# Nine loads moved from SP's queue to ACT's in a delta-rule attention with a softplus layer behind it

## The chip, the cores and the metric

The kernel runs on one core of a Trainium2 chip. The metric is device time in microseconds (us) of one execution, as the median of several. Beside the times there is one profiled execution, whose trace has every instruction of the five engines (PE for matmuls, DVE, ACT, POOL, and SP, which here only issues DMAs) and the landing of every DMA. Times inside a run are counted from the first instruction of the trace.

## What is computed

Four batches of eight heads go through a recurrence over 768 steps with a 48x48 state per head. The 384 features of each of the 3072 tokens then go through two dense layers with a softplus between them.

```python
k_n = k / (norm(k) + 1e-6)
for t in range(768):                       # q, k, v, g: [4, 8, 768, 48], beta: [4, 8, 768]
    y[:, :, t] = g[:, :, t] * (q[:, :, t] @ state)
    v_old = state^T k_n[:, :, t]
    state = state + beta[:, :, t] * outer(k_n[:, :, t], v[:, :, t] - v_old)
x = y as [3072, 384]
out = softplus(x @ w_in) @ w_out           # w_in: [384, 2048], w_out: [2048, 384]
```

## The kernel before

The 768 steps are cut into 12 chunks of 64, numbered 0 to 11, and all 32 heads are worked on together. For a chunk the kernel needs its keys, queries, values and gates. Each of these four is a tile of 384 KB, brought by two DMAs of 192 KB. Keys, values and gates arrive as 1024 rows of 192 bytes per DMA (`load`, L242 to L259, the DMA itself is at L249), queries as rows of 1536 bytes (`load_q`, L261 to L273, the DMA at L271). They land in rings of buffers: three for keys (`kf`), two for queries (`qf`), three for values (`vf`) and three for gates (`gf`). So a load waits until the last reader of the chunk that had the buffer before is done.

What reads them:

- A key tile is squared on ACT for the norm (`ksq`, L545), summed on DVE (`nv`, L549), and multiplied by the inverse norm on DVE or POOL (`kn`, L327), or only cast, in chunks 0 and 1. PE transposes the result and the query tile (L345, L388), ACT and DVE copy them out of PSUM (`kqt`), and PE multiplies them with each other (L503). ACT and DVE take the products out of PSUM (`kk` copies on ACT at L218, masks `mt` on DVE at L518).
- The inverse of each chunk's triangular matrix is built for two chunks at a time, on POOL for all pairs but the first (L629 to L646), and finished on PE (L707, L732, L770).
- The recurrence (`chain`) takes a value tile: DVE subtracts the readout (`w`, L847), PE multiplies twice (L855 and L878) with ACT or DVE copying in between and after (`u`, L218 or L220), PE updates the state (L898) and forms the output (L813, L928). DVE multiplies by the gate tile (`yg`, L943), PE transposes the product (L962), and ACT or DVE copies it (`xt`).
- The dense layers (`dense`) take `xt`: PE at L992, softplus on ACT (`ga`, L1004), PE at L1019, a copy out (`osb`) and the store by SP (L1039).

The weights of the dense layers are loaded by POOL's queue, eight DMAs in all (L297).

The order of everything is written out by hand. Each piece of work is an item with a number, and `_ORDER` is one long list of items, each with a letter for the engine that takes it: P, D, A, G (POOL) or S (SP). `emit` goes through the list once and records each item on its engine. Each engine then runs its own items strictly in that order, and waits between engines are put in where one item needs another's result or buffer. The list therefore fixes the order on each engine, not the times: an engine with little to do runs ahead of the others, as far as the buffers let it.

Loads are items too, eight per chunk: load 8c and 8c+1 are the two halves of the keys of chunk c, 8c+2 and 8c+3 the queries, 8c+4 and 8c+5 the values, 8c+6 and 8c+7 the gates. SP issues all of them but two key halves of chunks 0 and 1, which ACT issues as its first work.

One more rule comes with the recording layer. Loads and stores of SP and ACT count their landings on eight counters, taken in turn. A DMA that takes a counter waits, on the engine that issues it, until the DMA that had the counter before has landed. That one is eight places back among all loads and stores of both queues.

Of the kernel before, what the change touches and what calls it, by code (L numbers as in the profile page):

```python
# [37 lines left out]
class Program:  # L38
# [5 lines left out]
    def add(self, kind, tag, engs, fn, deps=(), bufs=(), mm=0, mode=None, size=0):  # L44
        it = Item()
        it.no, it.kind, it.tag, it.engs, it.fn = len(self.items), kind, tag, engs, fn
        it.deps = [d for d in deps if d is not None]
        it.bufs = list(dict.fromkeys(bufs))
        it.mm, it.mode, it.size = mm, mode, size
        for b in it.bufs:  # L50
            b.users += 1
        self.items.append(it)
        return it
# [21 lines left out]
def kernel(  # L75
# [12 lines left out]
    B, H, S, D = q.shape  # L88
# [19 lines left out]
    add = prog.add  # L108
# [133 lines left out]
    def load(name, x, r, c, b2):  # L242
        if (name, c) not in tiles:
            tiles[name, c] = (Buf(r), [])
        b, its = tiles[name, c]
        t0 = c * C

        def fn(en):
            ENG[en].dma_start(  # L249
                out=b.ap[64 * b2 : 64 * b2 + 64].rearrange("t p h d -> t (p h) d"),  # L250
                in_=x[2 * b2 : 2 * b2 + 2, :, t0 : t0 + C].rearrange(
                    "p h t d -> t (p h) d"
                ),
            )

        its.append(
            add("load", f"{name}{c}.{b2}", "A" if name == "k" and c < 2 and b2 else "S", fn,
                bufs=[b])
        )  # L259

# [14 lines left out]
    for c in range(NC):  # L275
        for b2 in range(2):
            load("k", k, r_k, c, b2)
        for m in range(2):
            load_q(c, m)
        for name, x, r in (("v", v, r_v), ("g", g, r_g)):  # L280
            for b2 in range(2):
                load(name, x, r, c, b2)
# [796 lines left out]
D162 D163 D164 D165 D166 D167 D168 D169 D170 D171 P128 S16 D172 D173 D174 P1251 D175 D176 D177  # L1079
P1244 A197 S25 D198 A222 P223 A224 G179 S11 A140 D178 G238 G239 P1245 A131 P1246 P1247 S24 A199  # L1080
P181 D180 S10 A139 P184 A182 D200 S4 D588 D132 D130 G188 A185 G187 P183 A190 P193 D194 A189 A594
P595 S13 A589 S32 P590 A201 D202 D203 D219 P186 A596 A591 P597 A598 P592 P605 A593 P603 S7 S6
D606 D604 A191 P204 P609 P607 A587 S34 D192 A275 D205 P209 D608 P214 S35 S42 S43 D211 A610 D210
D216 P220 G96 A212 A217 A215 D213 P141 A221 A142 A143 D218 D276 S41 S40 A277 P600 P599 D601 D602
P195 G300 D196 P872 D278 G99 A873 P230 A231 P225 A228 P1255 A226 A233 A235 D232 D229 D227 D611
D234 P874 A875 P886 D236 P619 P612 D620 D613 P151 D155 A284 P884 G98 A887 A885 G97 S14 D237 P285
P1254 A286 P882 P301 A883 A302 P615 A616 S49 P622 A623 P876 S15 A877 P878 G100 G101 G103 P614
P617 G279 D280 P621 P624 D153 S48 A879 A625 A618 G102 D281 P282 D297 P1252 D283 P630 D631 P632
D633 P292 A293 P298 A299 P880 A881 P634 A295 G240 G241 D294 D635 G242 G243 G244 G245 G246 P1253
G247 G248 P303 A304 G249 G250 G251 G252 G253 D306 D307 S50 P308 D296 A309 A311 P904 A905 P916  # L1090
A917 D312 P287 A290 D288 A313 P914 G254 G255 G256 D305 A915 P888 P910 A911 D314 D315 P627 P626
D629 D628 A353 D257 D258 P912 A913 P908 D354 P889 G259 D260 A909 G316 G317 P906 A907 G318 G319
G320 P902 A903 P890 P891 S57 A892 S56 P261 A262 G321 A267 P264 D265 A355 P895 P896 D291 P638
P266 P263 A270 D289 P643 P636 D310 G322 P897 P898 A268 P271 D356 G357 S20 S21 D644 A269 A899
P646 A647 D637 P639 A640 P918 S51 D362 P363 D272 A364 P641 A642 P645 P648 A649 S59 S58 A378 D358
P919 P920 P921 A922 D359 P650 P651 D653 P654 D652 S22 S23 D655 P656 P273 P925 P379 D657 A380
D274 P660 P667 P658 G323 G324 G325 G326 G327 A659 P926 P669 S28 S29 D668 G375 P670 A671 S65 S64
A431 D661 P663 D664 P927 D432 P672 A673 P662 P665 A666 S31 P360 D361 P376 S30 P678 D679 A377
P680 D681 P365 A366 D367 A368 D369 P928 P682 D683 P381 D383 A384 G328 G329 G330 G331 G332 G333
P386 A389 D388 D387 P956 S72 S73 A433 D385 A957 D434 P962 P370 D371 D390 D372 A963 A373 A382  # L1100
# [72 lines left out]
```

## Time and profile before

| what | value |
|---|---|
| median of 3 runs | 257.12 us (254.86 to 260.44) |
| the profiled execution | 255.46 us, of which the span from first to last instruction is 253.6 us |
| busy: PE, DVE, ACT, POOL | 236.9, 153.7, 153.0, 127.1 us |
| loads and stores on SP's queue | 23.2 MB, 50.2% of the 16 DMA engines' time |
| key, value and gate loads, from issue to landing | 3.4 us at least, 5.1 in the middle, 19.5 at most |
| one issue on SP, key loads | 595 ns at least, 639 in the middle, 5067 at most |
| mean granted clock of PE | 0.966 |

The profile's page gives busy times in 40 slices of the span, a digit for each in tenths; the row PEclk has the clock that PE was granted, and the row DMA the share of the DMA engines that was busy. The chain of work that ended last is followed back from the last instruction, at each step to whatever released it. The timelines list instructions by engine in order of time, with the start, the duration, the line, and in brackets the idle time ahead and what ended it. An engine's queue of DMA issues has a q behind its name (SPq, ACTq).

### The profile page before, as it was taken

The numbers are of one execution on the slowest core, as the hardware profiler recorded it, in microseconds if no ns is written. First come the engines' busy times: TensorE is split into PE (matmuls) and PEld (weight loads), VectorE is DVE, ScalarE is ACT, GpSimd is POOL, SyncE is SP. The second block draws the span as 40 slices with busy tenths as digits, with TensorE's granted clock in tenths as the row PEclk, the third lists the DMA queues.
The fourth block names the chain that finished last, engine by engine and source line by source line (L and its number), as shares of the span: only waits on it lengthen the run. The fifth ranks groups of instructions, "written<-read, shape, count | busy, mean of one in ns | idle before, by whom it ended". The sixth has DMA issues, their size and how long they took to land.

```text
span 253.6 us, 11355 instructions
## 1 busy us (share of the span) xinstructions
PE 236.9 (93%) x5040; PEld 160.5 (63%) x5040; DVE 153.7 (61%) x311; ACT 153.0 (60%) x285; POOL 127.1 (50%) x227
## 2 busy tenths in 40 slices
PE   7976588998989999999999999999999999999993
PEld 3543577676766765666766767755676565777751
DVE  7789888775893699759697588523843315313000
ACT  3557777686866579973777675456453475223530
POOL 8201653978879889988948859884000000000000
PEclk9999757799999999999999999999999999999999
DMA  8999999999990789083943850643024130112113
GB/s 111 198 181 178 178 179 180 186 195 176 176 153 6 173 180 157 4 200 83 156 98 84 170 99 22 124 83 80 3 66 93 23 80 0 34 32 48 34 47 78
DMA packets 86192, 27.56 MB, mean 109 GB/s; under 512 B 76288, under 2 KB 86144, under 8 KB 86144
## 3 DMA queue, kind: packets, MB, share of 16 engines
q1 hardware_dynamic: 80096, 23.21, 50.2%
q0 software_dynamic: 3968, 3.25, 8.2%
q10 hardware_dynamic: 2080, 0.39, 1.2%
q8 instruction: 39, 0.64, 1.2%
q14 instruction: 9, 0.07, 0.1%
HBM read 25.26 MB, written 4.72 MB: 118 GB/s over the span
## 4 chain that ended last, share of the span: by engine, by line
PE 76%; DVE 9%; DMA 4%; issue 3%; SPq 2%; ACT 2%; POOL 2%; ACTq 0%; DVEq 0%; POOLq 0%
PE h L992 25%; PE o L1019 23%; PE d L813 4%; DMA beta_l<-in_beta_dram 3%; PE d L855 3%; PE d L732 3%; PE d L770 3%; PE d L878 2%; PE d L928 2%; PE d L503 2%; PE d L707 2%; PE d L898 2%; PE d L388 2%; PE d L345 2%; POOL beta_l L175 2%
## 5 line engine op out<-in xcount | busy, mean ns | idle before, releaser
L1004 ACT ACTIVATE ga<-h 128x512 f16<-128x512 f32 x96 | 56.3, 598 | 33.4 <-PE h L992 27.6
L992 PE MATMUL h<-xt,w_in 128*128 128x512 f16 (+1 forms) x384 | 73.3, 330 | 0.1
L1019 PE MATMUL o<-w_out,ga 128*128 128x384 f16 x384 | 70.3, 326 | 1.4 <-issue 0.7
L1019 PEld LDWEIGHTS <-ga 128*128 128x128 f16 x384 | 35.7, 98 | 23.9 <-issue 1.8
L992 PEld LDWEIGHTS <-w_in 128*128 128x128 f16 x384 | 35.6, 99 | 20.7 <-issue 0.6
L639 POOL TENSOR_TENSOR tmp<-nn,tt 128x30 f32<-128x30 f32 (+7 forms) x75 | 30.1, 401 | 5.6
L646 POOL TENSOR_TENSOR tt<-tt,tmp 128x30 f32<-128x30 f32 (+7 forms) x75 | 29.4, 392 | 5.9
L566 POOL TENSOR_TENSOR nv<-nv,half_c 128x32 f32<-128x32 f32 x4 | 21.8, 5456 | 5.1 <-DVE nv L549 5.1
L218 ACT ACTIVATE kqt<-d 128x1024 f16<-128x1024 f16 (+1 forms) x21 | 18.4, 903 | 7.0 <-PE d L388 6.1
L218 ACT ACTIVATE osb<-o 128x384 f32<-128x384 f32 x18 | 8.8, 489 | 21.5 <-PE o L1019 21.4
L943 DVE TENSOR_TENSOR yg<-d,gf 128x384 f16<-128x384 f32 x24 | 12.8, 553 | 13.6 <-PE d L928 10.2
L1064 PE MATMUL o<-ident 128*128 128x512 f16 x72 | 19.3, 411 | 1.4 <-POOL ident masks.py:199 1.4
L847 DVE TENSOR_TENSOR w<-vf,d 128x384 f16<-128x384 f32 x22 | 11.3, 549 | 12.0 <-PE d L813 10.8
L218 ACT ACTIVATE u<-d 128x384 f16<-128x384 f32 x31 | 14.3, 491 | 7.1 <-PE d L878 3.3
L218 ACT ACTIVATE kk<-d 128x256 f16<-128x256 f32 (+1 forms) x34 | 12.8, 413 | 7.8 <-PE d L503 6.4
L518 DVE TENSOR_TENSOR mt<-d,mask 128x256 f16<-128x256 f32 x40 | 15.5, 418 | 3.2 <-PE d L503 1.9
L220 DVE CAST u<-d 128x384 f16<-128x384 f32 x17 | 9.1, 549 | 13.1 <-PE d L878 11.6
L813 PEld LDWEIGHTS <-kqt 48*64 48x64 f16 x704 | 13.3, 108 | 5.5 <-issue 5.3
L220 DVE COPY osb<-o 128x384 f32<-128x384 f32 x6 | 3.3, 556 | 21.6 <-PE o L1019 21.6
L813 PE MATMUL d<-s,kqt 48*64 48x48 f16 x704 | 16.4, 188 | 0.0
L545 ACT ACTIVATE ksq<-kf 128x768 f32<-128x768 f32 x12 | 10.1, 843 | 7.6 <-DMA kf<-in_k_dram 6.7
L220 POOL CAST tw<-tt 128x256 f16<-128x256 f32 x10 | 5.4, 563 | 16.1 <-DVE tt L646 16.0
(110 smaller groups left out, 380.1 us busy)
## 6 DMA issues: line engine op xcount, KB each, us to landing
qf<-in_q_dram SPq DMA_DIRECT2D x24, 192.0 KB, 5.1
vf<-in_v_dram SPq DMA_DIRECT2D x24, 192.0 KB, 5.2
gf<-in_g_dram SPq DMA_DIRECT2D x24, 192.0 KB, 4.2
out_dram<-osb SPq DMA_DIRECT2D x48, 96.0 KB, 2.4
kf<-in_k_dram SPq DMA_DIRECT2D x22, 192.0 KB, 5.1
w_in<-in_moe_w_in_dram POOLq DMA_DIRECT2D x4, 384.0 KB, 7.5
w_out<-in_moe_w_out_dram POOLq DMA_DIRECT2D x4, 384.0 KB, 12.9
kf<-in_k_dram ACTq DMA_DIRECT2D x2, 192.0 KB, 7.5
```

What stands on the lines that cost most here:

```text
L218: nc.scalar.activation(o, x, AF.Copy, scale=float(sign))
L220: ENG[en].tensor_copy(o, x)
L518: nc.vector.tensor_tensor(mt[c][m].ap[:, NP * p : NP * p + NP], gb[m].ap.rearrange("p (n b) -> p n b", n=NP)[:, :, C:], mask[:, None, :].b ...
L566: lambda en: nc.gpsimd.tensor_tensor(nv.ap, nv.ap, half_c, ALU.pow),
L639: eng.tensor_tensor(t, nn.ap[:, :, j + 1 :, j : j + 1].broadcast_to([P, 2, n, w]), tt.ap[:, :, j : j + 1, :w].broadcast_to([P, 2, n, w]), ...
L646: eng.tensor_tensor(rows, rows, t, ALU.add)
L813: nc.tensor.matmul(hd(o.ap)[HALF[r], NP * p + i], kq_of(c)[FEAT[m], 8 * p + 2 * i + r, off : off + C], s0[r].ap[FEAT[m], NP * p + i], **st ...
L943: lambda en, m=m: nc.vector.tensor_tensor(heads(yg.ap, m), hd(yp[m].ap), heads(gf.ap, m), ALU.mult),
L992: nc.tensor.matmul(hp.ap[:, n * b : n * b + n], w_in[:, j, f * P : (f + 1) * P], xt.ap[:, j, t0 : t0 + n], start=(j == 0), stop=(j == 2),)
L1004: lambda en, hp=hp, o=gb: nc.scalar.activation(o.ap, hp.ap, AF.Softplus),
L1019: nc.tensor.matmul(op.ap[:, :DM], b.ap[:, col + c0 : col + c0 + 128], w_out[:, f, :], start=(f == 0), stop=(f == NF - 1),)
L1064: nc.tensor.matmul(wb.ap.rearrange("p (a b) -> p a b", a=4), ident, ident[:, None, :].broadcast_to([P, 4, P]),)
```

## The change

Nine loads are recorded on ACT's queue in place of SP's. In the list only the letter changes from S to A, the place stays. In the order of the list they are: 32 (keys of chunk 4), 7 (gates of chunk 0), 41 (keys of chunk 5), 15 (gates of chunk 1), 48 (keys of chunk 6), 21 (values of chunk 2), 23 (gates of chunk 2), 29 (values of chunk 3) and 65 (keys of chunk 8). Each is one half of its tile; the other half stays with SP. In `load` the engines that an item may take are widened for this. Nothing else differs: PE, DVE and POOL have the same instructions in the same order, ACT has nine issues more and SP nine fewer. Since the counters are taken in turn over both queues, and the recording layer sorts the issues of the two by its own reckoning, some loads come to wait for another load than before.

```diff
         its.append(
-            add("load", f"{name}{c}.{b2}", "A" if name == "k" and c < 2 and b2 else "S", fn,
+            add("load", f"{name}{c}.{b2}", "A" if name == "k" and c < 2 and b2 else "SA" if c < 9 else "S", fn,
                 bufs=[b])
         )
...
-P595 S13 A589 S32 P590 A201 D202 D203 D219 P186 A596 A591 P597 A598 P592 P605 A593 P603 S7 S6
+P595 S13 A589 A32 P590 A201 D202 D203 D219 P186 A596 A591 P597 A598 P592 P605 A593 P603 A7 S6
 D606 D604 A191 P204 P609 P607 A587 S34 D192 A275 D205 P209 D608 P214 S35 S42 S43 D211 A610 D210
-D216 P220 G96 A212 A217 A215 D213 P141 A221 A142 A143 D218 D276 S41 S40 A277 P600 P599 D601 D602
+D216 P220 G96 A212 A217 A215 D213 P141 A221 A142 A143 D218 D276 A41 S40 A277 P600 P599 D601 D602
...
-P1254 A286 P882 P301 A883 A302 P615 A616 S49 P622 A623 P876 S15 A877 P878 G100 G101 G103 P614
-P617 G279 D280 P621 P624 D153 S48 A879 A625 A618 G102 D281 P282 D297 P1252 D283 P630 D631 P632
+P1254 A286 P882 P301 A883 A302 P615 A616 S49 P622 A623 P876 A15 A877 P878 G100 G101 G103 P614
+P617 G279 D280 P621 P624 D153 A48 A879 A625 A618 G102 D281 P282 D297 P1252 D283 P630 D631 P632
...
-P266 P263 A270 D289 P643 P636 D310 G322 P897 P898 A268 P271 D356 G357 S20 S21 D644 A269 A899
+P266 P263 A270 D289 P643 P636 D310 G322 P897 P898 A268 P271 D356 G357 S20 A21 D644 A269 A899
...
-P919 P920 P921 A922 D359 P650 P651 D653 P654 D652 S22 S23 D655 P656 P273 P925 P379 D657 A380
-D274 P660 P667 P658 G323 G324 G325 G326 G327 A659 P926 P669 S28 S29 D668 G375 P670 A671 S65 S64
+P919 P920 P921 A922 D359 P650 P651 D653 P654 D652 S22 A23 D655 P656 P273 P925 P379 D657 A380
+D274 P660 P667 P658 G323 G324 G325 G326 G327 A659 P926 P669 S28 A29 D668 G375 P670 A671 A65 S64
```

In these lines A277 and A431 are the `ksq` of chunks 5 and 8, D606 and D604 the `yg` of chunk 0, D644 one half of the `w` of chunk 2, and D668 one half of the `w` of chunk 3.

## The prediction

> **What bounds the kernel now.** I read the busy slices first, then the chain that ended last, then the timelines of ACT, DVE and SP around the nine places.
>
> From the page, busy tenths in slices of 6.3 us:
>
> ```profile
> PE   7976588998989999999999999999999999999993
> ...
> ACT  3557777686866579973777675456453475223530
> ...
> PEclk9999757799999999999999999999999999999999
> DMA  8999999999990789083943850643024130112113
> ```
>
> From about 40 us on PE is full to the end: what makes PE wait there is not won back. The DMA engines are full up to 76 us and have room after it.
>
> The chain of work that ended last, in the window 28 to 60 us (start, us, what):
>
> ```profile
> 34.04 0.89 PE d L878 x32
> 34.93 0.02 issue
> 34.95 0.50 ACT u L218
> 35.45 0.33 issue
> 35.78 0.40 DVE yg L943
> ```
>
> ACT's copies of u and the product yg, which reads the gate tile of chunk 0, are themselves on the chain. A load put on ACT's queue in front of them, or a gate that comes late, costs the end directly.
>
> SP's timeline, where the loads are issued (start, us, what):
>
> ```profile
> 25.04 2.10 SPq L249 DMA_DIRECT2D gf<-in_g_dram  x2
> ...
> 33.92 1.33 SPq L249 DMA_DIRECT2D kf<-in_k_dram  x2
> ```
>
> and ACT's timeline beside it:
>
> ```profile
> 34.53 0.92 ACT L218 ACTIVATE u<-d 128x384 f16<-128x384 f32 x2 [0.79 <-PE d L878]
> ...
> 39.95 2.00 ACT L218 ACTIVATE kqt<-d 128x1024 f16<-128x1024 f16 x3
> 41.81 0.86 ACT L545 ACTIVATE ksq<-kf 128x768 f32<-128x768 f32 x1
> ```
>
> This is the heart of it. In the order table load 7 (a gate of chunk 0) stands after the u copies and load 41 (a key of chunk 5) after the kqt copies. SP issues them at 25.04 and 33.92, because SP carries only DMAs and runs ahead of the table. ACT reaches the same places at 35.45 and 41.95. "The same place in the order" is 8 to 20 us later in time.
>
> **What is removed.** Nine issues leave SP, about 0.65 us each (min 595, median 639 to 712 ns): 6 us of a queue that is idle for long stretches. That is worth nothing by itself. SP's later loads move up, but most wait for a buffer (9.2 us once, for DVE's kn), and those waits stay.
>
> **What is added, place by place.** An ACT issue occupies ACT 0.71 to 0.80 us (the two key loads that ACT issues at 1.0 us). From the start of an issue to the landing of the load takes 3.4 us at least, 3.6 for the load at 82.01 into a quiet queue, 4.8 for the one at 33.92, 11.9 for that at 35.30 and 19.5 for that at 38.23, when the weights pass on POOL's queue. A is when ACT gets there in the profile of before, R the first reader and its time.
>
> - Load 32 (key, chunk 4): A 31.6, R ksq 37.23. It lands near 36, in time. Its 0.75 us stand before the sqrt and the u copy at 32.01; the second u copy, which PE needs, loses some 0.5. **+0.5** (0 to 0.8).
> - Load 7 (gate, chunk 0): A 35.45, plus the 0.5 to 0.75 just lost: starts at 36.2. R is yg at 35.78, on the chain. Quiet, it lands at 39.8, by the load at 33.92 at 41.0, by that at 35.30 at 48.1. Weights are moving then: counting packets of 45 to 53 us, SP's queue gets 175 to 203 in a us beside POOL's 179 to 202, and 152 to 177 from 41 to 45; so a load's 1024 packets take 5 to 7 us, after some 2 of start. I take 45: **+9** (4 to 12). Behind yg on DVE stand to, kqt, xt and the masks; PE's transposes of yg (L962, 36.88), next in its order, wait for it, and ACT's xt for those.
> - Load 41 (key, chunk 5): A 41.95, R ksq at 41.81, the very next ACT instruction. ACT itself now sits through the latency: 3.6 quiet, 11.9 at worst. By then, 9.5 us later than now, most of the weights are through; I take **+5.5** (3.6 to 9). Behind it on ACT: the first softplus, then the kk copies that free PSUM for PE.
> - Load 15 (gate, chunk 1): A 54.4, R yg at 57.92, which already waits 1.0 us for it. It lands 3.6 to 4.9 after its issue: **+0.7** (0 to 1.5). Load 48 (key, chunk 6) is read 10 us later: 0.
>
> After 76 us the DMA engines are quiet, so 3.6 counts:
>
> - Load 21 (value, chunk 2): A 75.8, lands 79.4; R w on DVE at 74.73, and PE takes that up at 77.62: **+2.5** (1 to 4.5).
> - Load 23 (gate, chunk 2): A 82.94, lands 86.5; R yg at 83.98. PE's transposes move from 85.59 to 87.6, and ACT's xt from 86.13 to 88.1.
> - Load 29 (value, chunk 3) stands right after that xt: starts at 88.9, lands at 92.5; R w at 85.70, so PE's umm at 86.83 starts at 93.1, and ACT's u copy behind it ends at 94.15 instead of 87.89. It also waits, on ACT, until a load of chunk 9, eight DMAs back, has landed (85.65 now): in time.
> - Load 65 (key, chunk 8) follows that u copy, and ksq is next on ACT: it starts at 94.15, and ksq at 97.75 instead of 87.79. The u copies behind it go from 88.82 to 98.6; PE's L928 at 90.17, which had 0.4 to spare, waits for them. The three loads follow one another, so their delays add: **+9.4** (5 to 12).
>
> **The clock.** PE's granted clock is half from 28.0 to 41.7 us and again from 45.1 to 48.5, after a gap of 1.34 us in PE; that is one step of 3.4 us. In the half step twelve h matmuls took 2.38, outside it six took 0.66. So a step costs up to 1.7 us. Five of the waits above are over 2 us; not all of a step is PE's own time. **+4** (0 to 9). The Trainium skill, "TensorE: Matmul & The Clock Gate" (Part 1, the HAM clock gate), has the same: an idle window of about 3.4 us brings half rate. By its wording gaps shorter than the window would cost nothing, and the term would be near 2; this trace shows a drop after 1.34, so I keep 4.
>
> **The sum.** 0.5 + 9 + 5.5 + 0.7 + 2.5 + 9.4 + 4 = 31.6 us, on the profiled execution's own 255.5 (span 253.6): **287 us**. That execution lies inside the three runs of 254.9 to 260.4, 1.6 under their median; so against the median of 257.1 I say 12% slower. 2%, some 5 us, is what a measurement of this kernel can tell from no change.
>
> **The rivals.**
>
> *The waits overlap or find cover.* All nine latencies are near 3.6, the DVE and ACT delays hide in each other, and the clock stays: 0 + 4 + 3.6 + 0 + 1 + 5 = 13.6, so 269 us; with less still, 262 to 273. For it: ACT is busy 60% and DVE 61%. Against it: after 40 us PE has hardly a gap to hide in.
>
> *Two queues beat one (faster).* Where the weights pass, packets of POOL's queue and SP's alternate one for one. A third queue gets its own share, so keys and gates gain on the weights. The place is 37 to 58 us: the gate issued at 38.23 lands at 57.73, and yg waits 1.0 for it; PE lost 1.34 at 43.36 and 0.71 at 57.20. All of that won is 3 us, and were the half clock of 45 to 48.5 us gone too, 1.7 more: 251. It decides only if a load from ACT lands within 0.3 us of ACT's arrival for load 7 and at once for 41, against the 3.4 us that is the least of all key, value and gate loads. The Trainium skill, "DMA: Bandwidth & Descriptors" (Queues, rings and completion order), has this rule, an engine going round the queues packet by packet; the counts above agree.
>
> *Nothing changes.* The latencies were prefetched far enough, only issue time moves: 255 to 258. The Trainium skill, "DMA: Bandwidth & Descriptors" (Issuing engines are not separate DMA queues), speaks for this: all queues share the 16 engines, and another issuer saves only the sequencer's time. It is silent on what stands behind the issue. The table itself speaks against: for 7, 41, 21, 23, 29 and 65 the reader comes within 2 us of ACT's arrival, or before it.
>
> *Heavier.* Load 7 and 41 each meet the full 12 us of 35.30, the clock takes 9: 0.8 + 12 + 9 + 1.5 + 4.5 + 12 + 9 = 49, so 304.
>
> **The chances.** The forecast (273 to 300) 0.70; overlap (262 to 273) 0.15; heavier 0.07; no change 0.05; faster 0.03. The range of 268 to 302 leaves out both small cases, part of the overlap and the heavy end. Faster by over 2%: 0.03; within 2%: 0.05; slower: 0.92.
>
> **What would show it.** In the profile after: yg's first instruction waits on a DMA of gf for 5 us or more near 36 us; ksq on ACT waits on kf twice, after 41 and near 90 or later, 3 us or more each; w waits on vf twice; ACT's queue issues nine more loads, each soon after the ACT instruction ahead of it; PEclk shows more half steps before 110 us; and from there to the end the two timelines run in parallel. I am wrong if yg of chunk 0 doesn't wait, or if PE finds other work while ACT waits, which its fixed order forbids.

## The result, and the profile after

The changed kernel takes 288.66 us (median of 4 executions, 285.73 to 292.26) against 256.96 us for the kernel before (254.86 to 260.44): 1.123 times the time, with an interval of 1.108 to 1.137. The execution that was profiled took 289.54 us, its span is 287.8 us. That is 34.2 us more span than before. Of every kernel some executions come out a few us longer than the rest: the ratios and the differences in us below leave them out, and so do the times of late4 and splate7, but the traces of late4, three and splate7 are of such executions.

Four parts of the page, first the busy slices (7.2 us each now), then the loads' two queues (packets, MB, share of 16 engines), the chain by engine and the line of DMA issues on ACT's queue:

```profile
PE   8965804689996942599999999999999999999993
...
ACT  3657723386964520269856786753644447423530
...
PEclk9999555859999795569999999999999999999999
DMA  8999799809971497800359637416322413012122
```

```profile
q1 hardware_dynamic: 70736, 21.44, 41.9%
...
q10 hardware_dynamic: 11440, 2.16, 5.0%
...
PE 62%; DMA 16%; POOL 9%; DVE 8%; issue 2%; ACT 1%; DVEq 0%; ACTq 0%; POOLq 0%
...
kf<-in_k_dram ACTq DMA_DIRECT2D x6, 192.0 KB, 5.7
```

The loss stands mostly in two holes of PE's row, slices 6 to 8 and 15 to 17, and in and around each of them the clock is at half. From slice 18 on both kernels are full to the end. DMA holds 16% of the chain. In the kernel before it held 4%, and PE 76%:

```profile
PE 76%; DVE 9%; DMA 4%; issue 3%; SPq 2%; ACT 2%; POOL 2%; ACTq 0%; DVEq 0%; POOLq 0%
```

No byte more is moved: 9360 packets went from SP's queue (q1) to ACT's (q10).

The first hole, in the chain of work that ended last, window 28 to 60 us (start, us, what):

```profile
33.19 0.90 PE d L878 x16
34.09 0.02 issue
34.12 0.01 ACT u L218
34.12 11.24 DMA gf<-in_g_dram
...
45.55 0.06 DVE yg L943
...
50.56 5.95 DMA kf<-in_k_dram
...
56.67 0.85 ACT ksq L545
```

Read it downwards: the u copy starts on ACT at 34.12, load 7 behind it is issued in the same instant, and the next thing that the kernel's end hangs on is its landing 11.24 us later, and then yg. The same again with load 41, 5.95 us, and `ksq`.

The waits in the window 28 to 130 us (who waited for whom; us in total, times, the longest):

```profile
DVE yg L943 <- DMA gf<-in_g_dram: 14.0, 2, 10.5
...
DVE w L847 <- DMA vf<-in_v_dram: 11.0, 2, 6.7
...
PE d L962 <- DVE yg L943: 10.4, 1, 10.4
ACT ksq L545 <- DMA kf<-in_k_dram: 10.3, 2, 5.4
...
PE d L855 <- DVE w L847: 9.0, 2, 6.3
```

In the kernel before only one of these three waits for a DMA was there:

```profile
DVE yg L943 <- DMA gf<-in_g_dram: 1.0, 1, 1.0
```

Since PE executes the same 5040 matmuls in the same order in both kernels, the loss can be followed matmul by matmul: how much later does each start than in the kernel before? This distance is worked out from the two traces, with the times of the kernel before on the left:

```
before, us   matmul                              later by, us
  32.86      umm (L855)                              -0.8
  36.88      transposes of yg, chunk 0 (L962)        +9.8   load 7
  47.27      h (L992)                                +8.6
  47.48      h, waits for ACT's softplus            +10.6   load 41
  51.59      h (L992)                               +13.2   half clock, 0.6 of it softplus
  76.03      o (L1019)                              +12.2
  77.62      umm, chunk 2 (L855)                    +15.1   load 21
  79.42      L878                                   +16.5   half clock
  85.28      behind the transposes of yg, chunk 2   +19.6   load 23
  86.92      umm, chunk 3 (L855)                    +26.3   load 29
  88.99      L878                                   +27.8   half clock
  89.63      behind the u copies after ksq, chunk 8 +31.4   load 65
  93.31      h (L992)                               +33.9   half clock
  the end                                           +34.2
```

### The profile page after: what moved, and what is told of

It is laid out like the page before. It is cut to its first block, busy times and chain, and to the rows that moved or that the text cites. A ratio compares the mean times of both kernels' runs of the same rounds, so it can differ in the third digit from the quotient of the medians.

```text
span 287.8 us, 11351 instructions
## 1 busy us (share of the span) xinstructions
PE 245.3 (85%) x5040; PEld 166.2 (58%) x5040; DVE 153.6 (53%) x311; ACT 153.5 (53%) x285; POOL 127.7 (44%) x227
## 4 chain that ended last, share of the span: by engine, by line
PE 62%; DMA 16%; POOL 9%; DVE 8%; issue 2%; ACT 1%; DVEq 0%; ACTq 0%; POOLq 0%
PE o L1019 21%; PE h L992 19%; DMA gf<-in_g_dram 6%; DMA kf<-in_k_dram 4%; DMA vf<-in_v_dram 4%; PE d L813 3%; DMA beta_l<-in_beta_dram 3%; POOL tt L646 2%; PE d L855 2%; PE d L732 2%; PE d L878 2%; POOL tmp L639 2%; PE d L928 2%; POOL nv L566 2%; PE d L707 2%
## 5 line engine op out<-in xcount | busy, mean ns | idle before, releaser
L1019 PE MATMUL o<-w_out,ga 128*128 128x384 f16 x384 | 72.0, 333 | 0.6 <-ACT osb L218 0.6
L646 POOL TENSOR_TENSOR tt<-tt,tmp 128x30 f32<-128x30 f32 (+7 forms) x75 | 32.6, 435 | 5.9
L639 POOL TENSOR_TENSOR tmp<-nn,tt 128x30 f32<-128x30 f32 (+7 forms) x75 | 27.3, 364 | 5.6
L847 DVE TENSOR_TENSOR w<-vf,d 128x384 f16<-128x384 f32 x22 | 11.3, 549 | 22.6 <-PE d L813 11.3
L1064 PE MATMUL o<-ident 128*128 128x512 f16 x72 | 19.5, 413 | 1.4 <-POOL ident masks.py:199 1.4
L813 PE MATMUL d<-s,kqt 48*64 48x48 f16 x704 | 17.3, 191 | 2.7 <-DVE yg L943 2.7
L813 PEld LDWEIGHTS <-kqt 48*64 48x64 f16 x704 | 14.1, 111 | 8.3 <-issue 8.1
L855 PE MATMUL d<-w,te 64*64 64x48 f16 x384 | 10.2, 195 | 9.1 <-DVE w L847 9.0
L549 DVE TENSOR_REDUCE nv<-ksq 128x16 f32<-128x768 f32 x12 | 11.3, 939 | 10.3 <-ACT ksq L545 10.1
```

Source lines behind the costliest of these rows:

```text
L639: eng.tensor_tensor(t, nn.ap[:, :, j + 1 :, j : j + 1].broadcast_to([P, 2, n, w]), tt.ap[:, :, j : j + 1, :w].broadcast_to([P, 2, n, w]), ...
L646: eng.tensor_tensor(rows, rows, t, ALU.add)
L813: nc.tensor.matmul(hd(o.ap)[HALF[r], NP * p + i], kq_of(c)[FEAT[m], 8 * p + 2 * i + r, off : off + C], s0[r].ap[FEAT[m], NP * p + i], **st ...
L855: nc.tensor.matmul(hd(up.ap)[HALF[r], pi], td.ap[HALF[r], 16 * cl + 2 * pi + m], w1.ap[HALF[r], pi],)
L1019: nc.tensor.matmul(op.ap[:, :DM], b.ap[:, col + c0 : col + c0 + 128], w_out[:, f, :], start=(f == 0), stop=(f == NF - 1),)
L1064: nc.tensor.matmul(wb.ap.rearrange("p (a b) -> p a b", a=4), ident, ident[:, None, :].broadcast_to([P, 4, P]),)
```

## The experiments

Two theories were on trial. The first, of the prediction: a load on ACT is issued only when ACT gets to its place in the list, so it starts 8 to 20 us later than on SP, and its reader waits out a whole transfer. The rival: ACT's queue itself is to blame, either because its loads are served worse or because the issues hold up ACT's own work. Every kernel below has the widened line in `load`, as the changed kernel has it; only its lines of the list are shown. All ratios are against runs of the kernel before on the same chip. Of only7, only41, only65, eight and fill8 there are two executions each, of late4 and splate7 one time each.

### One load at a time: 7, 41, and 65

```diff
-P595 S13 A589 S32 P590 A201 D202 D203 D219 P186 A596 A591 P597 A598 P592 P605 A593 P603 S7 S6
+P595 S13 A589 S32 P590 A201 D202 D203 D219 P186 A596 A591 P597 A598 P592 P605 A593 P603 A7 S6
```

> Load 7 (a gate of chunk 0) alone on ACT, the other eight on SP. By lateness (ACT reaches the place at 34 to 35 us, SP issued at 25): yg of chunk 0 waits for the gate as in the changed kernel, PE is 9 to 11 us behind from L962 on, half-clock steps in and after the wait add 0 to 2: 264 to 269 us. By occupancy (an issue costs ACT its 0.6 us and nothing else): 255 to 258. By shared queues (what counts is how many loads go on the second queue): a ninth of the 32 us, 259 to 260.

Measured: 267.45 us, 1.045 (1.039 to 1.051), 11.0 us more than before. The load is issued at 34.55 and lands 12.10 us later. DVE's timeline (in brackets the wait):

```profile
46.77 1.02 DVE L943 TENSOR_TENSOR yg<-d,gf 128x384 f16<-128x384 f32 x2 [11.53 <-DMA gf<-in_g_dram]
```

PE's transposes of yg stand at +11.0. At 57.91 us of the kernel before the distance is down to +7.9, at 76.03 it is up again at +10.7, and at the end of the trace it is +11.3. One load makes a third of the loss, and by the end nothing of it is won back.

```diff
-D216 P220 G96 A212 A217 A215 D213 P141 A221 A142 A143 D218 D276 S41 S40 A277 P600 P599 D601 D602
+D216 P220 G96 A212 A217 A215 D213 P141 A221 A142 A143 D218 D276 A41 S40 A277 P600 P599 D601 D602
```

> Load 41 (a key of chunk 5) alone on ACT. By lateness: ksq on ACT waits 5 to 9 us (the weights pass now at 42 us, as they did not in the changed kernel where the wait fell at 52), PE covers about 2 of it with h matmuls, a half-clock step or two: 259 to 265. By occupancy: 255 to 258. By shared queues: 259 to 260.

Measured: 264.55 us, 1.034 (1.028 to 1.040), 8.1 us more. ACT's timeline has the issue and the wait behind it:

```profile
39.94 0.60 ACTq L249 DMA_DIRECT2D kf<-in_k_dram  x1
...
52.09 0.84 ACT L545 ACTIVATE ksq<-kf 128x768 f32<-128x768 f32 x1 [10.44 <-DMA kf<-in_k_dram]
```

PE jumps by 7.4 us where an h matmul waits for the first softplus, which stands behind `ksq` on ACT.

```diff
-D274 P660 P667 P658 G323 G324 G325 G326 G327 A659 P926 P669 S28 S29 D668 G375 P670 A671 S65 S64
+D274 P660 P667 P658 G323 G324 G325 G326 G327 A659 P926 P669 S28 S29 D668 G375 P670 A671 A65 S64
```

> Load 65 (a key of chunk 8) alone on ACT. It is issued near 87.5 us, when SP sends the keys, queries and values of chunks 9, 3 and 4 (DMA engines 0.9 busy there in the kernel before). By lateness with that traffic: ksq on ACT waits 5 to 7 us, PE is 3.5 to 6 us behind after it and 1 to 2 of half clock come on top: 260 to 264. With a quiet queue, as the prediction had it: ksq waits 3.6, 258 to 260. If the four late loads cost what they cost alone and just add up, this one is 3.6 plus half clock of the 22.6 us of the run with the four.

Measured: 262.81 us, 1.026 (1.016 to 1.035), 6.7 us more. Issued at 87.37, landed after 5.1 us:

```profile
92.59 0.84 ACT L545 ACTIVATE ksq<-kf 128x768 f32<-128x768 f32 x1 [4.74 <-DMA kf<-in_k_dram]
```

PE is 4.2 us late behind it, and 5.7 to 6.1 once a half step of the clock has passed. So even alone, with no other load moved, the latency here isn't the 3.6 us that the prediction took for a quiet stretch.

### The last four, and the three that should cost nothing

```diff
-P266 P263 A270 D289 P643 P636 D310 G322 P897 P898 A268 P271 D356 G357 S20 S21 D644 A269 A899
+P266 P263 A270 D289 P643 P636 D310 G322 P897 P898 A268 P271 D356 G357 S20 A21 D644 A269 A899
...
-P919 P920 P921 A922 D359 P650 P651 D653 P654 D652 S22 S23 D655 P656 P273 P925 P379 D657 A380
-D274 P660 P667 P658 G323 G324 G325 G326 G327 A659 P926 P669 S28 S29 D668 G375 P670 A671 S65 S64
+P919 P920 P921 A922 D359 P650 P651 D653 P654 D652 S22 A23 D655 P656 P273 P925 P379 D657 A380
+D274 P660 P667 P658 G323 G324 G325 G326 G327 A659 P926 P669 S28 A29 D668 G375 P670 A671 A65 S64
```

> Loads 21, 23, 29 and 65 alone on ACT, all read after 73 us. By lateness the four waits of the changed kernel come back one behind the other: 2.9 + 3.1 + 6.7 + 3.6 at PE and 4 to 6 of half clock, 20 to 22 in all, and nothing before 74 us: 274 to 280. By the sizes of the prediction (3.6 us from issue to landing): 2.5 + 9.4 + 2, 268 to 271. By occupancy: 255 to 259. By shared queues: 4/9 of 32, 269 to 271 with the loss spread evenly.

Measured: 277.18 us, 20.8 us over the 256.41 of the kernel before. The waits in the profile: w on values 11.6 us in two, yg on gates 5.6, `ksq` of chunk 8 on keys 5.8. One wait was not expected: `ksq` of chunk 5 waits 5.44 us at 46.52, for a key load that SP issued at 34.13 and that took 12.3 us; in the kernel before the same load, issued at 34.58, took 5.1. PE stands at +2.0 at 76.03 of the kernel before, and at +26.4 at the end. In the trace of the changed kernel PE goes from +12.2 to +34.2 over the same stretch, 22.0 us. The four loads are about two thirds of the loss.

```diff
-P595 S13 A589 S32 P590 A201 D202 D203 D219 P186 A596 A591 P597 A598 P592 P605 A593 P603 S7 S6
+P595 S13 A589 A32 P590 A201 D202 D203 D219 P186 A596 A591 P597 A598 P592 P605 A593 P603 S7 S6
...
-P1254 A286 P882 P301 A883 A302 P615 A616 S49 P622 A623 P876 S15 A877 P878 G100 G101 G103 P614
-P617 G279 D280 P621 P624 D153 S48 A879 A625 A618 G102 D281 P282 D297 P1252 D283 P630 D631 P632
+P1254 A286 P882 P301 A883 A302 P615 A616 S49 P622 A623 P876 A15 A877 P878 G100 G101 G103 P614
+P617 G279 D280 P621 P624 D153 A48 A879 A625 A618 G102 D281 P282 D297 P1252 D283 P630 D631 P632
```

> Loads 32, 15 and 48 alone on ACT: ACT reaches them early enough for their readers, by 4 to 10 us, or the reader waited for them before as well. By lateness: no waits, 253 to 257, and the 1.0 us wait of yg of chunk 1 gone or smaller. By occupancy: plus 0 to 2, 255 to 259. By shared queues: a third of the 32 us, 265 to 268.

Measured: 257.31 us, 0.999 (0.995 to 1.004), by the medians 0.1 us more. Loads 32, 15 and 48 cost nothing that this interval would show. This speaks against the second half of the rival: three issues on ACT, one of them ahead of the u copies on the chain, add up to less than the interval. The profiled execution, 259.27 us, has a wait that the kernel before has not:

```profile
45.59 0.84 ACT L545 ACTIVATE ksq<-kf 128x768 f32<-128x768 f32 x1 [3.83 <-DMA kf<-in_k_dram]
```

As in late4 it is for a key load of chunk 5 from SP's queue: issued at 34.80, it took 10.7 us, where the kernel before had both of these loads issued from 33.92 on and landed in 4.8 and 5.1. So what a load among the weights takes differs by 7 us with neither its queue nor its place in the list changed. In late4 no load ahead of 74 us is moved, so such a wait comes without the change too.

The Trainium skill, "DMA: Bandwidth & Descriptors" (Issuing engines are not separate DMA queues), says that issuing from several engines saves only the time that a sequencer takes to start the DMAs. These three agree; the other six show what that sentence leaves out.

### The same delay without ACT's queue

Here load 7 stays on SP. ACT writes one column of the gate tile at the place where the changed kernel has the load, and the load waits for that, since it overwrites the column. Five loads that stood behind it in SP's order (6, 34, 35, 42 and 43) go ahead of it; those that stay behind it, the keys of chunk 5 first, start later too, at 36.35 us in place of 33.92.

```diff
+    late = add("touch", "", "A",
+               lambda en: nc.scalar.activation(
+                   tiles["g", 0][0].ap[64:, 0, 0, :1], half_c[64:, :1], AF.Copy),
+               bufs=[tiles["g", 0][0]])
...
-P595 S13 A589 S32 P590 A201 D202 D203 D219 P186 A596 A591 P597 A598 P592 P605 A593 P603 S7 S6
-D606 D604 A191 P204 P609 P607 A587 S34 D192 A275 D205 P209 D608 P214 S35 S42 S43 D211 A610 D210
+P595 S13 A589 S32 P590 A201 D202 D203 D219 P186 A596 A591 P597 A598 P592 P605 A593 P603 S6 S34 S35 S42 S43 A1256 S7
+D606 D604 A191 P204 P609 P607 A587 D192 A275 D205 P209 D608 P214 D211 A610 D210
```

> No load on ACT's queue but the two of the kernel before. Load 7 stays on SP's queue but is made late: ACT writes one column of the gate tile behind its u copies (about 0.2 us more on ACT, overwritten by the load), SP's load waits for that and so starts near 35.6 us in place of 25. The loads that stood behind it in SP's order and wait for nothing (6, 34, 35, 42, 43) go ahead of it. By lateness: yg of chunk 0 waits until the load lands, 4.8 to 11.9 us after its start by the loads issued around there before, 261 to 269. By the queue itself: 255 to 259.

Measured: 264.45 us, 8.4 us over the 256.05 of the kernel before. The issue in SP's timeline and the reader in DVE's:

```profile
35.64 0.61 SPq L249 DMA_DIRECT2D gf<-in_g_dram  x1
...
46.62 1.02 DVE L943 TENSOR_TENSOR yg<-d,gf 128x384 f16<-128x384 f32 x2 [11.12 <-DMA gf<-in_g_dram]
```

The load takes 10.8 us from SP where it took 11.2 to 12.1 from ACT, yg waits 11.12 us, and PE's transposes stand at +10.8. To this wait the queue makes no difference that shows; the moment of the issue does. The whole time is 2.6 us less than with load 7 alone on ACT (8.4 against 11.0 us); with a single time and SP's order changed, this stays open.

### ACT's queue without the delay

The other way round: all nine loads go by ACT, but each at an earlier place in the list, near the time at which SP issued it.

```diff
-P1244 A197 S25 D198 A222 P223 A224 G179 S11 A140 D178 G238 G239 P1245 A131 P1246 P1247 S24 A199
+P1244 A197 S25 D198 A222 P223 A32 A224 A7 G179 S11 A140 D178 G238 G239 P1245 A131 P1246 P1247 S24 A199
...
-P595 S13 A589 S32 P590 A201 D202 D203 D219 P186 A596 A591 P597 A598 P592 P605 A593 P603 S7 S6
+P595 S13 A589 P590 A201 D202 D203 D219 P186 A596 A591 P597 A41 A598 P592 P605 A593 P603 S6
...
```

Likewise 15 stands before A191, 48 before A277, 21 before A877, 23 before A879, 29 before G259 and 65 before P264.

> All nine loads on ACT's queue as in the changed kernel, but recorded earlier in ACT's order, where ACT comes by at about the time that SP issued them: load 32 near 23 us, 7 near 24.5, 41 near 34, 15 near 35, 48 near 41.8, 21 and 23 near 55, 29 near 67, 65 near 72. By lateness: none of the waits for gates, keys and values of the changed kernel is left, 253 to 259. By the queue itself (loads on ACT's queue land late or hold ACT up, wherever they stand): 270 to 289.

Measured: 254.92 us, 0.995 (0.992 to 0.998). ACT issues at 21.8, 24.0, 33.8, 35.0, 40.1, 53.2, 53.9, 66.0 and 72.2 us. In the timelines neither yg of chunk 0 nor `ksq` of chunk 5 waits for a load, and DVE's only wait for one between 28 and 130 us is the one that the kernel before had too:

```profile
35.84 1.02 DVE L943 TENSOR_TENSOR yg<-d,gf 128x384 f16<-128x384 f32 x2 [1.21 <-ACT u L218]
...
41.87 0.86 ACT L545 ACTIVATE ksq<-kf 128x768 f32<-128x768 f32 x1
```

```profile
DVE w L847 <- DMA gf<-in_g_dram: 0.9, 1, 0.9
```

Nine loads on ACT's queue, and the 31 us are gone. This settles the dispute. The time lay below that of the kernel before, so the same kernel was measured again.

> The same kernel as in the run with all nine loads recorded earlier, to settle its small difference from the kernel before. If the 0.5% is real: ratio 0.993 to 0.998, 254 to 256. If it was chance: the interval includes 1.

Measured: 254.95 us, 0.996 (0.993 to 0.999). The gain of 0.4% is small, but twice on its own side of one. This version is no slower than the kernel before, and perhaps half a percent faster. Where the gain comes from was looked for with load 15 alone, the gate for which yg of chunk 1 waited 1.0 us before:

```diff
-D606 D604 A191 P204 P609 P607 A587 S34 D192 A275 D205 P209 D608 P214 S35 S42 S43 D211 A610 D210
+D606 D604 A15 A191 P204 P609 P607 A587 S34 D192 A275 D205 P209 D608 P214 S35 S42 S43 D211 A610 D210
...
-P1254 A286 P882 P301 A883 A302 P615 A616 S49 P622 A623 P876 S15 A877 P878 G100 G101 G103 P614
+P1254 A286 P882 P301 A883 A302 P615 A616 S49 P622 A623 P876 A877 P878 G100 G101 G103 P614
```

> Load 15 (a gate of chunk 1) alone on ACT, recorded where ACT is at 35 us; yg of chunk 1 waited 1.0 us for it in the kernel before, which had it land at 57.7 behind four other loads on SP's queue. If the gain of the nine early loads is this one wait: 0.5 to 1 us, ratio 0.995 to 0.998. If it comes from the others: 0.998 to 1.002.

Measured: 256.07 us, 0.997 (0.993 to 1.001). The interval holds one, so it stays open whether this load is the source.

### Do the delays add?

The single costs are 11.0 (7), 8.1 (41), 20.8 (the last four) and 0.1 (the three): 40.0 us, but the changed kernel loses 31.0 (287.78 against 256.80). So the changed kernel was run with load 7 back on SP:

```diff
-P595 S13 A589 A32 P590 A201 D202 D203 D219 P186 A596 A591 P597 A598 P592 P605 A593 P603 A7 S6
+P595 S13 A589 A32 P590 A201 D202 D203 D219 P186 A596 A591 P597 A598 P592 P605 A593 P603 S7 S6
```

> The changed kernel with load 7 back on SP. If the delays add: 288.7 less the 10.6 that load 7 alone costs, 276 to 280. If the price of a late load is the traffic that it meets: without the 10 us of load 7, load 41 is issued at 40 us into the weights again, as alone (7.7 us), and not at 50.6 behind them; then 256.8 + 7.7 + 22.6, 284 to 288, and load 7 was nearly free in the changed kernel.

Measured: 284.73 us, 1.113 (1.108 to 1.118), 28.7 us over the 256.05 before. The sum of the singles without load 7 is 29.0. So these eight add, and load 7, worth 11.0 alone, is worth 2 to 3 on top of them. The overlap is with load 41, as ACT's timeline shows here:

```profile
41.50 0.60 ACTq L249 DMA_DIRECT2D kf<-in_k_dram  x1
...
53.42 0.84 ACT L545 ACTIVATE ksq<-kf 128x768 f32<-128x768 f32 x1 [10.71 <-DMA kf<-in_k_dram]
```

and in the changed kernel:

```profile
50.56 0.60 ACTq L249 DMA_DIRECT2D kf<-in_k_dram  x1
...
56.67 0.84 ACT L545 ACTIVATE ksq<-kf 128x768 f32<-128x768 f32 x1 [4.96 <-DMA kf<-in_k_dram]
```

With load 7 out of the way, load 41 is issued 9 us earlier, in the middle of the weights, and ACT waits 10.71 us, 7.9 of which PE loses. Behind a late load 7 it is issued after most of the weights have passed, ACT waits 4.96, and PE loses 2.0. At 76.03 us of the kernel before the two stand at +8.9 and +12.2: the 3.3 us that separate them.

### The clock term

To keep PE's clock up during the wait for load 7, eight groups of three idle matmuls were put ahead of the transposes of yg in the changed kernel.

```diff
-    IDLE = 24
+    IDLE = 32
...
-D606 D604 A191 P204 P609 P607 A587 S34 D192 A275 D205 P209 D608 P214 S35 S42 S43 D211 A610 D210
+D606 D604 A191 P204 P1256 P1257 P1258 P1259 P1260 P1261 P1262 P1263 P609 P607 A587 S34 D192 A275 D205 P209 D608 P214 S35 S42 S43 D211 A610 D210
```

> The changed kernel with eight more groups of idle matmuls on PE (24 matmuls of 128x512, 5 to 11 us) ahead of the transposes that wait for yg of chunk 0, so within the 9.8 us of that wait. By the clock (the half steps are a part of the price): the clock goes up before the wait ends and PE's distance to the kernel before is 1 to 3 us smaller after it, 285 to 288. If the clock costs nothing there: 288 to 290.

Measured: 291.30 us, 1.138 (1.134 to 1.143), not less than the changed kernel's 1.123. That is outside both expectations. The clock was full from 36.7 to 47.0 us, where it had been half throughout from 28.2 to 52.0. But load 7 landed 13.7 us after its issue instead of 11.2, so DVE made yg later:

```profile
47.96 1.02 DVE L943 TENSOR_TENSOR yg<-d,gf 128x384 f16<-128x384 f32 x2 [12.80 <-DMA gf<-in_g_dram]
```

The idle matmuls had ended at 41.7, so they held nothing up, but at 47.0 the clock fell to half again, before yg, and stayed there until 53.8. The work behind the wait thus met the half clock as in the changed kernel, and the transfer varies by more than the term that was to be measured. So the run did not test what it was made for, and what the half clock costs in this hole stays open. What the half steps cost elsewhere is read from the changed kernel's trace alone, in the next section.

## Why the prediction was right

287 us were forecast, 288.66 measured, and the mechanism is the one named: the letter in the list decides whose progress the issue hangs on, and with it the moment. What was to show it is there: yg waits 10.48 us (5 or more were named), `ksq` twice, 4.96 and 5.38 (3 or more), w twice, 4.33 and 6.67, and from 93 us of the kernel before to the end the two run in parallel, +33.9 and +34.2. Its steps, against the distances above:

| term | predicted | in the trace |
|---|---|---|
| load 32 | 0.5 | -0.8 |
| load 7 | 9 | 10.6 |
| load 41 | 5.5 | 2.0, and 4.96 of wait on ACT |
| load 15 | 0.7 | -0.4 |
| load 21 | 2.5 | 2.9 |
| loads 23, 29, 65 | 9.4 | 3.1 + 6.7 + 3.6 = 13.4 |
| half clock | 4 | 2.7 + 1.5 + 1.5 + 2.5 = 8.2, of which 0.6 is a wait for softplus |

These terms give 35.9, and the small drifts between them, gains of PE's own in stretches without a wait, bring it to the 34.2 of the whole trace. Most of the -0.8 is a wait of 0.63 us ahead of umm that PE has in the kernel before and not here; no run ties it to load 32. Three terms were mis-sized, and the errors partly cancelled: that the total came within 2 us is in part luck. So is the landing of load 7. It was put at 45 us, by an issue at 36.2 and 8.8 us of latency; the issue came at 34.12, beside the second u copy and not behind it, and the load took 11.24 us, so it landed at 45.4.

**Load 41 was too dear.** The step "ACT itself now sits through the latency" holds: 4.96 us. That PE had "hardly a gap to hide in" does not hold here: it went on through its h matmuls and lost 2.0. In all three traces shown here with load 41 at this place PE covers about 3 us of ACT's wait: it waits 1.9 us against ACT's 4.96 here, 7.3 against 10.44 in only41 and 7.9 against 10.71 in eight. Taken alone (1.034) the load costs more than was forecast for it; the term is small because load 7 comes first, which makes the wait short.

**The last three were too cheap.** The step that failed is "after 76 us the DMA engines are quiet, so 3.6 counts". It misread the page's slice row, in which the DMA share is 0 from 76 to 82 us but 7, 8 and 9 tenths in the three slices behind it. A table of windows of the kernel before shows the same (PE, PEld, DVE, ACT and POOL busy with counts, granted clock, DMA share, GB/s):

```profile
76.00:82.00 6.00, 5.97 (x141) 4.32 (x141) 2.60 (x5) 4.25 (x8) 5.84 (x4) 1.00 0.03 7
82.00:92.00 10.00, 10.00 (x326) 7.70 (x325) 7.19 (x14) 6.04 (x11) 8.67 (x20) 1.00 0.75 168
92.00:98.00 6.00, 5.95 (x107) 2.96 (x105) 6.00 (x15) 5.29 (x11) 5.66 (x10) 1.00 1.01 169
```

The quiet lasts six microseconds, until at 82 DVE's `kn` frees a key buffer and SP, which had been waiting for it, issues a burst of its own. In the changed kernel that burst starts at 95.75, and the same view has

```profile
86.00:96.00 10.00, 7.23 (x200) 5.26 (x200) 5.28 (x11) 3.99 (x8) 8.56 (x7) 0.85 0.11 21
96.00:106.00 10.00, 7.27 (x209) 5.58 (x209) 2.70 (x5) 4.12 (x7) 8.07 (x18) 0.98 0.82 170
106.00:116.00 10.00, 3.72 (x69) 2.22 (x68) 1.58 (x3) 1.22 (x2) 4.28 (x9) 0.53 0.80 132
```

Load 21, issued at 87.63, falls into the quiet stretch, takes 4.3 us and fits its term. Loads 23, 29 and 65, at 99.16, 105.92 and 113.91, fall into the burst and take 5.0, 6.7 and 5.8. That they follow one another and add, as forecast, shows in DVE's timeline: each wait starts only after the one before it has ended.

```profile
92.07 1.02 DVE L847 TENSOR_TENSOR w<-vf,d 128x384 f16<-128x384 f32 x2 [4.33 <-DMA vf<-in_v_dram]
...
104.29 1.02 DVE L943 TENSOR_TENSOR yg<-d,gf 128x384 f16<-128x384 f32 x2 [3.52 <-DMA gf<-in_g_dram]
...
112.64 1.02 DVE L847 TENSOR_TENSOR w<-vf,d 128x384 f16<-128x384 f32 x2 [6.67 <-DMA vf<-in_v_dram]
```

**The clock cost nearly twice its term.** In the changed kernel it is half from 28.2 to 52.0, 58.9 to 65.7, 93.0 to 96.4 and 106.7 to 127.1 us. The first group of the next two lines is from the kernel before, the second from the changed one, the same six matmuls:

```profile
51.26 0.82 PE L992 MATMUL h<-xt,w_in 128*128 128x256 f16 x6
```

```profile
64.18 1.48 PE L992 MATMUL h<-xt,w_in 128*128 128x256 f16 x6
```

1.48 against 0.82 us, with no wait in between. The four rises in the distance, in stretches at half clock, make 8.2 us, or 7.6 without the 0.6 for which PE waits there on a second softplus. This is a reading of one trace; the attempt to take the half steps away did not separate them.

**Load 32 and the price of an issue.** The prediction charged 0.71 to 0.80 us of ACT for an issue ahead of the u copies. At load 32 ACT's timeline shows none of it paid:

```profile
29.93 0.47 ACT L226 ACTIVATE to<-d,own 128x256 f16<-128x256 f32 x1 [0.47 <-PE d L732]
30.05 0.60 ACTq L249 DMA_DIRECT2D kf<-in_k_dram  x1
30.31 0.47 ACT L226 ACTIVATE te<-d,own 128x256 f16<-128x256 f32 x1
30.66 0.93 ACT L218 ACTIVATE w<-vf 128x384 f16<-128x384 f32 x2
```

The issue runs beside the ACTIVATE of 29.93. The three behind that one, te and two w, stand ahead of the load in the list, start after it was issued, and follow each other without a gap. The kernel with the three harmless loads (0.999) says the same in time. Behind load 7 a part is paid:

```profile
34.12 0.62 ACTq L249 DMA_DIRECT2D gf<-in_g_dram  x1
34.79 0.47 ACT L226 ACTIVATE te<-d,own 128x256 f16<-128x256 f32 x1 [0.18 <-issue]
```

In the kernel before te follows the u copies without a gap, at 35.34. Here it starts 0.18 us after them and 0.05 us after the end of the issue. It is the same in only7 (0.19), in fill8 (0.17) and in early9, where load 15 stands at this place (0.19); eight and only41, with no issue there, have no gap. So in these rows an issue is hidden as long as ACT has something older to run, and here only the last 0.2 to 0.3 us of the 0.62 show.

Of the rivals, "nothing changes" holds for three of the nine loads, "the waits overlap" for the pair 7 and 41 alone, and "two queues beat one" gives no gain in this kernel as changed: it would have needed load 7 to land within 0.3 us of ACT's arrival, and it took 11.2. In the version with the earlier places a small gain shows, 0.4%; whether a second queue or merely another order of the loads makes it was not tried.

## What to carry to other kernels

A prefetch is worth the distance between its issue and its reader, and the place in a hand-written list is no measure of that distance when the queue changes: find the time at which the new issuer reaches the place, not the place. If a load has to go by a computing engine, move it up by as much as the old queue ran ahead. And before one counts a latency as "quiet", the DMA share of the very window has to be looked up, and the bursts in it moved along with the delay, since a burst that waits for a buffer comes later with it.

## What was not expected

- **An issue on ACT costs ACT 0 to 0.3 us, not its 0.6.** The issue at 30.05, of 0.60 us, overtook three ACTIVATEs that are ahead of it in the list, and held none of them up; behind the one at 34.12, which had only a u copy to run beside, the next ACTIVATE came 0.2 to 0.3 us late. The Trainium skill, "TensorE: Matmul & The Clock Gate" (the table ahead of its first section), gives ScalarE a queue eight deep that is strictly in order; a sequencer that runs ahead of the engine by some places agrees with this row, though no run here measured its depth.
- **The same load of 1024 rows of 192 bytes takes 3.4 to 19.5 us.** Among the weights on POOL's queue load 7 takes 11.2, 12.1, 13.7 (ACT) and 10.8 us (SP), and five loads that SP issues from 33.92 to 38.23 us in the kernel before take 4.8 to 19.5. In SP's burst it is 5.0 to 6.7, in the quiet stretch 4.3. Within this spread no difference between ACT and SP as issuers stands out.
- **Of delays in a row the first can pay for the next.** Load 7 is worth 11.0 us alone and 2 to 3 with load 41 behind it, because its delay moves the issue of load 41 out of the traffic.
